# Order of w_in steps, reciprocals and sums in couples 1 to 6 of a fused attention and feed-forward kernel

## The chip, the cores and the metric

The kernel runs on one core of a Trainium2 chip. The metric is the device time of one execution in microseconds (us). Engines are called TensorE (PE in the profile; PEld is its weight load), VectorE (DVE), ScalarE (ACT), GpSimd (POOL) and SyncE (SP, which issues most DMAs).

## What is computed

```
q, k, v: (8, 12, 448, 64) float32;  g_q, g_k: (64,)
q_n = q / sqrt(mean(q*q) + 1e-6) * g_q;   k_n likewise
attn = softmax(q_n @ k_n^T / 8);          o = attn @ v
x = o, heads side by side                 # (3584, 768)
h = x @ w_in;  out = silu(h) @ w_out      # w_in (768, 2048), w_out (2048, 768)
```

w_in and w_out arrive with 8 bytes per element and are rounded to 4 on the chip.

## The kernel before, in words

**Couples.** Two pairs of heads (four heads of one batch) make a couple. There are NC = 24 couples; the code counts them c = 0 to 23, so "couple 1" in the title is c = 0 and "couple 6" is c = 5. GROUP = 6 couples hold two batches, after which the products with w_in for those two batches can run. EARLY is 5, LATE 12, LEFT 3: the 448 keys are three blocks of 128 (j = 0, 1, 2) and a rest of 64 per head (j = LEFT).

**Order.** Nothing is scheduled by a planner. The order of the program text is the order in each engine's queue; an instruction waits by semaphores for its inputs and for the readers of what it overwrites. `visit(c)` writes out the attention of couple c: `scores` (TensorE, then the exponential on ACT, L714), `weigh` (exponentials times v, L746), `add` (DVE, L760: adds blocks of exponentials for the softmax sum). It starts with the end of couple c - 1: `weigh` of its LEFT and last blocks, then a copy of the two results out of PSUM into x (L1393), or from c - 1 = 5 on `divide` at once. `beside` is the RMS normalisation of couple c + 1, in four pieces: squares on ACT (L464), reductions on DVE (L465), roots and scaling on POOL (L493, L508).

`between(c)` follows: q transposes of c + 1 (`transpose_q`, L626), the softmax sums of c (`sum_up`, products with ones, L780, into one PSUM tile `t`), k transposes of c + 1 (`transpose_k`, L644), and `fill`, which deals out products of the feed-forward part (L882) with other work between them.

**Reciprocals.** `sum_up` yields twice: after the first block's products, and with a list of two steps when all sums are issued. The steps are `invert(0)` and `invert(1)`, one reciprocal on DVE for each half of `t` (L789, into r[0]), and `spread`, six DMAs that copy rows of r so that both pairs' factors are in place: four (L795) that read what invert wrote, then two (L797) that overwrite part of what these read, and so wait for them. `divide` multiplies x by r (L804). For c = 0 to 2 these steps are kept in `inverting` and run in the middle of visit(c + 1), after the division of couple c - 1. For c = 3 and 4 they are dealt out in the second `fill` of between(c), after the division of c - 1. For c = 5 they run in between(5), also after it.

**PSUM.** Eight banks: "sc", two tiles of two banks (scores and transposes, in turn); "av0" and "av1", one bank each (sums of `weigh`); "mm", two tiles of one bank (feed-forward products; `bank` hands them out). The tile `t` of `sum_up` comes from `bank` for c < 6, and from "sc" after that.

**w_in.** `Rounder` takes 24 pieces of 128 x 512 through load (DMA), `open` (two ACT instructions, L100 and L101) and `round` (three on DVE, L123 to L130, one add on POOL, L134, and up to two further loads). `weights_in(c, half)` gives the steps of a half couple, "r" for a rounding and "o" for an opening; it also gives calls of `sum_w_in(i, step)`, one DVE operation on 128 x 768 (L837 or L840) that builds sums of blocks of w_in for a seven-product scheme. Chunk 0 needs its four steps before the products of between(6).

**Early products.** `make_ahead`, begun in between(3), computes two products each for the first two row blocks (L882); they are dealt out in five shares, one in between(3) and two each in between(4) and between(5). A product of `mm` is copied by ACT (L890) or added by DVE (L840) before its bank is free.

**SP's queue** in a couple: the q load (L268), `spread`, "vrest" loads (L326, L329), the v load for the next couple (L313), k loads (L289, L293), w_in loads (L85).

Of the kernel before, what the change touches and what calls it, by code (L numbers as in the profile page):

```python
# [11 lines left out]
F32 = mybir.dt.float32  # L12
# [15 lines left out]
BANK = 512  # L28
# [504 lines left out]
def bounded(  # L533
# [3 lines left out]
    P, D, R, J, S = z.P, z.D, z.R, z.J, z.S  # L537
# [5 lines left out]
    ps = others.enter_context(tc.tile_pool(name="ps", bufs=1, space=bass.MemoryType.PSUM))  # L543
# [3 lines left out]
    GROUP, LATE = z.NPAIR, z.LATE  # L547
# [152 lines left out]
    def scores(c, j, i=None):  # L700


        two = ps.tile([P, 2, BANK], F32, name="sc", bufs=2)
        for half in range(2):
            pair = half if j == LEFT else i
            keys = kT[:, ds((z.KA, z.KB)[0 if j == LEFT else i] + j * P, P)]
            for h in range(2):
                rows = ds(h * D, D)
                nc.tensor.matmul(  # L709
                    two[ds(half * D, D), h, 0:S], keys[rows, ts(half, D)], qT[rows, pair, :],  # L710
                    start=True, stop=True,
                )
        for h in range(2):
            nc.scalar.activation(  # L714
                eleft[:, h] if j == LEFT else weights(c, j)[:, i, h], two[:, h, 0:S], AF.Exp,
                scale=norm.column(c, i, h, j),
            )
# [46 lines left out]
    def sum_up(c):  # L764

        n = D // 2
        early = c < GROUP  # L770
        t = bank(S) if early else ps.tile([P, 2, BANK], F32, name="sc", bufs=2)[:, 0, 0:S]
        terms = [(0, lambda: weights(c, 0))]
        if early:
            terms = [(0, lambda: weights(c, LEFT - 1))] + terms + [(1, None)]
        for k, (which, w) in enumerate(terms):
            if k == len(terms) - 2:
                yield
            for h in range(2):
                for i in range(2):
                    nc.tensor.matmul(  # L780
                        t[ds(h * D + i * n, n), :],
                        ones[:, which + i if which else 0],
                        eleft[:, h] if which else w()[:, i, h],
                        start=(k == 0), stop=(k == len(terms) - 1),
                    )

        def invert(half):
            rows = ts(half, S // 2)
            nc.vector.reciprocal(out=r[0][:, rows], in_=t[:, rows])  # L789

        def spread():
            mine = [a.rearrange("(h i p) s -> i h p s", h=2, i=2) for a in r]
            for i in range(2):
                for h in range(2):
                    nc.sync.dma_start(mine[1][i, h], mine[0][1, h])  # L795
            for h in range(2):
                nc.sync.dma_start(mine[0][1, h], mine[0][0, h])  # L797

        yield [lambda: invert(0), lambda: (invert(1), spread())]

    def divide(c, source):
        for i in range(2):
            x = x_of(c, i)
            nc.vector.tensor_tensor(  # L804
                out=x, in0=x if source is None else source[i], in1=r[i], op=ALU.mult
            )
# [55 lines left out]
    def bank(n):  # L862
        turn = turns["next"] = (turns["next"] + 1) % 4
        if ps_alone is None or turn == 0:
            return ps_mm.tile([P, BANK], F32, name="mm")[:, 0:n]
        return ps_alone.tile([P, BANK], F32, name="alone")[:, 0:n]
# [486 lines left out]
    step_of = {"o": lambda: room.w_in.open(), "r": lambda: room.w_in.round()}  # L1353
    halves = {0: "ro", 1: "ro", 2: "ro", 3: "roo", 4: "or", 5: "or", 6: "or", 7: "oroo"}
    visits = {GROUP + 2: "rr", GROUP + 4: "rr"}
    sums_halves = {-6: [(0, 0)], -5: [(0, 1)], -4: [(0, 2)], -3: [(0, 3)]}
    sums_halves[8] = [(3, step) for step in range(4)]
    sums_visits = {GROUP + 1: 1, GROUP + 3: 2}

    def weights_in(c, half):  # L1360
        i = 2 * (c - GROUP) + half
        work = [step_of[step] for step in ("ro" if c < GROUP else halves.get(i, ""))]
        return work + [lambda a=a: sum_w_in(*a) for a in sums_halves.get(i, ())]

    def weights_in_visit(c):
# [9 lines left out]
    def visit(c):  # L1375

        beside = normalise(c + 1) if c <= GROUP else []
        if c < NC:
            scores(c, 0, 0)
        run_all(beside[0:1])  # L1380
        if c > 0:
            weigh(c - 1, LEFT)
            weigh(c - 1, LEFT - 1, 0)
            turn(1, nc.scalar.copy if c <= GROUP else nc.vector.tensor_copy)
        if c < NC:
            scores(c, 0, 1)
        if c == 0:
            run_all(beside[1:2])
        if c > 0:
            weigh(c - 1, LEFT - 1, 1)  # L1390
            if c - 1 < EARLY:
                for i in range(2):
                    nc.vector.tensor_copy(x_of(c - 1, i), sums[i])  # L1393
                run_all(beside[1:2])
                if inverting:
                    if c > 1:
                        divide(c - 2, None)
                    run_all(inverting)
                    inverting.clear()
            else:  # L1400
                divide(c - 1, sums)
                run_all(beside[1:2])
                if c < NC and c % GROUP == 0:
                    for i in range(0 if c == GROUP else 1, HW):
                        sum_x(last_two(c), i)
                weights_in_visit(c)
            if c + 1 < NC:
                loads["vrest"](c + 1)
        if c == NC:
            return  # L1410
        scores(c, 1, 0)
        scores(c, 1, 1)
        if c < GROUP:
            run_all(beside[2:3])
        weigh(c, 0, 1)
        scores(c, 2, 0)
        weigh(c, 1, 1)
        turn(0, nc.scalar.copy)
        if c < GROUP:
            run_all(beside[3:4])  # L1420
        scores(c, 2, 1)
        weigh(c, 0, 0)
        run_all(add(c, 1))
        weigh(c, 1, 0)
        scores(c, LEFT)
        if c + 1 < NC:
            loads["v"](c + 1)

    def run_all(work):
        for piece in work:  # L1430
            piece()

    def between(c):

        def transposes_and_sums():
            summing = sum_up(c)
            if c < GROUP:
                next(summing)
            if c < LATE - 1:
                transpose_k(c + 1)  # L1440
            reciprocals = next(summing)
            if LATE - 1 <= c < NC - 1:
                reciprocals += [lambda: flip(c + 1, "k"), gain]
            if GROUP // 2 <= c <= EARLY:
                divide(c - 1, None)
            return reciprocals

        if c < LATE - 1:
            transpose_q(c + 1)
        elif c < NC - 1:  # L1450
            flip(c + 1, "q")
        if c < GROUP // 2:
            inverting.extend(transposes_and_sums())
        elif c == GROUP - 1:
            run_all(transposes_and_sums())
        if c >= GROUP and c % GROUP == 0:
            fetched = range(AHEAD) if c == GROUP else ()
            columns = products - 2 * HW * S * len(fetched)
            work = halves_in(last_two(c), range(HF), plain_in, dict(begun), fetched)
            begin(work, columns, 2 * GROUP)  # L1460
            begun.clear()
        late = add(c, LEFT - 1) + add(c, LEFT) if c >= GROUP else []
        further = normalise(c + 2) if c >= GROUP - 1 else []
        fill(late + weights_in(c, 0) + further[2:])
        prompt = transposes_and_sums() if GROUP // 2 <= c != GROUP - 1 else []
        if c == GROUP // 2:
            begin(make_ahead([0, 1]), AHEAD * 2 * HW * S, GROUP - 1)
        if c >= LATE - 2:
            if c == LATE - 2:
                prompt.append(pair_up)  # L1470
            queries = prompt[3:] + [lambda: sum_squares(c + 2)]
            fill(weights_in(c, 1), prompt[:3] + [lambda: run_all(queries)])
        else:
            fill(weights_in(c, 1) + (further[:2] if c >= GROUP else []), prompt)
        if c % GROUP == GROUP - 1:
            finish()
            if c == GROUP - 1:
                begun[0] = fetch_ahead([0, 1], 0)
            else:
                sum_x([c // GROUP * 2, c // GROUP * 2 + 1], 0)  # L1480
        if c >= LATE - 2:
            scale(c + 2)
        if GROUP <= c < NC - 1:

            nc.scalar.activation(first, minus_half, AF.Exp)
        if c == NC - 1:
            while rounder.load():
                pass

    begun, inverting = {}, []  # L1490
# [234 lines left out]
```

## Time and profile before

| | us |
|---|---|
| median of 3 runs | 1331.43 (1331.42 to 1336.38) |
| profiled execution, whole time | 1333.6 |
| its span | 1331.8 |
| TensorE busy | 1301.7 (98%) |
| DVE busy | 942.2 (71%) |
| ACT busy | 506.6 (38%) |
| POOL busy | 363.8 (27%) |

The span is what the profiler saw of the program; the whole time is 1.8 us longer. Busy shares are averages over the whole span: attention of the first six couples takes about the first 130 us, a stretch without the large feed-forward products. In timelines a row has its start, its duration, the engine, the line, the operation with what it writes and reads, and in brackets the idle time before it and what ended it. Merged rows ("x2") cover several instructions. "Q" after an engine (SPq) marks what its instruction queue does, such as issuing DMAs.

### The profile page before, as it was taken

Reading aid. Unit: us, or ns where it says so; the run is one execution under the profiler, and the core shown is the slowest. Engines: PE = TensorE matmul, PEld = TensorE weight load, DVE = VectorE, ACT = ScalarE, POOL = GpSimd, SP = SyncE. Lnnn points to the kernel's source line nnn. Section 1 sums busy time; section 2 is a strip of 40 time slices with the busy share of each in tenths; the row PEclk is TensorE's granted clock in tenths of the full one; section 3 lists DMA queues with packets and bytes.
Section 4 is the critical chain, followed back from the end, with each engine's and each line's share of the span. In section 5 each row is a group of like instructions: output and inputs, shape, how many; then the busy total and the mean of one; then the engine's idle time right before and its main releaser. Section 6 shows DMA issues by size and latency. Waiting matters only on the chain.

```text
span 1331.8 us, 19793 instructions
## 1 busy us (share of the span) xinstructions
PE 1301.7 (98%) x7189; PEld 833.1 (63%) x7189; DVE 942.2 (71%) x1623; ACT 506.6 (38%) x890; POOL 363.8 (27%) x229
## 2 busy tenths in 40 slices
PE   8998999999999999999999999999999999999998
PEld 4333444444444444444444455557999999999998
DVE  5787777785755555854554586688978787878785
ACT  7876556655454554455545244410001000001000
POOL 5765534344333433433330154410000000000000
PEclk9999999999999999999999999999999999999999
DMA  8564436333444444444321257522323232332311
GB/s 231 149 167 134 119 98 168 103 89 94 95 94 115 98 93 117 94 94 115 88 66 62 97 179 249 171 74 76 99 76 99 76 105 83 97 105 71 127 48 39
DMA packets 249487, 144.94 MB, mean 109 GB/s; under 512 B 184292, under 2 KB 233316, under 8 KB 249380
## 3 DMA queue, kind: packets, MB, share of 16 engines
q1 hardware_dynamic: 248816, 142.60, 38.0%
q8 instruction: 59, 0.97, 0.3%
q0 software_dynamic: 256, 0.79, 0.2%
q14 instruction: 48, 0.39, 0.1%
q10 hardware_dynamic: 308, 0.20, 0.1%
HBM read 93.98 MB, written 41.29 MB: 102 GB/s over the span
## 4 chain that ended last, share of the span: by engine, by line
PE 84%; DVE 7%; ACT 3%; issue 3%; DMA 2%; POOL 1%; SPq 0%; ACTq 0%; DVEq 0%; POOLq 0%
PE mm L882 26%; PE alone L1189 22%; PE av L746 8%; PE sc L709 7%; PE mm L1189 7%; PE alone L882 7%; PE alone L1226 2%; DVE work L760 1%; PE sc L780 1%; DVE work L789 1%; DVE sums_x L837 1%; DMA work<-work 1%; PE mm L1226 1%; PE sc L644 1%; PE sc L626 0%
## 5 line engine op out<-in xcount | busy, mean ns | idle before, releaser
L882 PE MATMUL mm<-x,W 128*128 128x448 f32 x636 | 256.7, 546 | 6.1 <-DVE parts L840 2.3
L714 ACT ACTIVATE work<-sc,rms 128x448 f32<-128x448 f32 x324 | 184.7, 633 | 81.0 <-PE sc L709 64.9
L882 PEld LDWEIGHTS mm<-x,W 128*128 128x128 f32 x636 | 116.7, 190 | 138.0 <-issue 109.0
L882 PE MATMUL mm<-sums_x,W 128*128 128x448 f32 x456 | 183.7, 543 | 1.6 <-DVE parts L840 1.6
L709 PE MATMUL sc<-work 64*64 64x448 f32 x1344 | 168.2, 549 | 2.6 <-ACT work L714 1.4
L746 PE MATMUL av<-work,rows 64*64 64x448 f32 x1296 | 156.6, 543 | 6.3 <-ACT av L722 1.8
L760 DVE TENSOR_TENSOR work<-work 128x896 f32<-128x896 f32 (+1 forms) x114 | 123.7, 1118 | 49.3 <-PE av L746 48.7
L493 POOL TENSOR_TENSOR rms<-rms,minus_half 128x14 f32<-128x14 f32 (+4 forms) x43 | 106.4, 2476 | 149.8 <-DVE rms L489 140.2
L882 PEld LDWEIGHTS mm<-sums_x,W 128*128 128x128 f32 x456 | 85.1, 190 | 90.7 <-issue 82.8
L520 POOL DMA_DIRECT2D out_dram<-x x2 | 1.3, 653 | 443.2 <-DVE x L840 443.2
L1189 PE MATMUL alone<-W,rows 128*128 128x192 f32 x608 | 113.0, 326 | 0.0
L746 PEld LDWEIGHTS av<-work,rows 64*64 64x64 f32 x1296 | 59.9, 133 | 78.0 <-issue 35.5
L709 PEld LDWEIGHTS sc<-work 64*64 64x64 f32 x1344 | 55.2, 134 | 73.8 <-ACT work L714 27.6
L1189 PEld LDWEIGHTS alone<-W,rows 128*128 128x128 f32 x608 | 101.2, 190 | 0.0
L902 POOL TENSOR_TENSOR parts<-parts,stage 128x448 f32<-128x448 f32 x31 | 42.0, 1356 | 148.7 <-DVE parts L840 148.4
L685 POOL TENSOR_TENSOR rms<-rms,minus_half 128x28 f32<-128x28 f32 x12 | 57.5, 4794 | 67.2 <-DVE rms L682 58.0
L1189 PE MATMUL alone<-W,work 128*128 128x192 f32 x382 | 72.2, 326 | 0.0
L1020 ACT ACTIVATE stage<-stage 128x896 f32<-128x896 f32 x63 | 57.3, 945 | 24.1 <-DVE stage L840 23.4
L465 DVE TENSOR_REDUCE rms<-rows 128x8 f32<-128x512 f32 (+2 forms) x56 | 35.9, 641 | 42.5 <-ACT rows L464 38.9
L1189 PEld LDWEIGHTS alone<-W,work 128*128 128x128 f32 x382 | 63.8, 190 | 0.0
L1199 ACT COPY rows<-alone 128x192 f32<-128x192 f32 x34 | 10.8, 317 | 137.8 <-PE alone L1189 79.0
L789 DVE RECIPROCAL work<-sc 128x224 f32<-128x224 f32 x36 | 55.7, 1548 | 5.2 <-PE sc L780 5.0
(244 smaller groups left out, 2115.4 us busy)
## 6 DMA issues: line engine op xcount, KB each, us to landing
hidden<-stage SPq DMA_DIRECT2D x63, 448.0 KB, 3.0
work<-hidden SPq DMA_DIRECT2D x21, 1024.0 KB, 5.0
rows<-in_moe_w_out_dram SPq DMA_DIRECT2D x32, 384.0 KB, 3.3
W<-in_moe_w_in_dram SPq DMA_DIRECT2D x22, 512.0 KB, 5.2
work<-work SPq DMA_DIRECT2D x144, 56.0 KB, 2.0
x<-hidden SPq DMA_DIRECT2D x7, 1024.0 KB, 6.1
rows<-in_q_dram SPq DMA_DIRECT2D x96, 56.0 KB, 2.2
rows<-in_k_dram SPq DMA_DIRECT2D x96, 56.0 KB, 2.3
```

Of the source, the lines that this page charges most:

```text
L493: nc.gpsimd.tensor_tensor(out=t, in0=t, in1=half, op=ALU.pow)
L685: nc.gpsimd.tensor_tensor(out=f, in0=f, in1=minus_half.to_broadcast([P, n]), op=ALU.pow)
L709: nc.tensor.matmul(two[ds(half * D, D), h, 0:S], keys[rows, ts(half, D)], qT[rows, pair, :], start=True, stop=True,)
L714: nc.scalar.activation(eleft[:, h] if j == LEFT else weights(c, j)[:, i, h], two[:, h, 0:S], AF.Exp, scale=norm.column(c, i, h, j),)
L746: nc.tensor.matmul(sums[i][ds(h * D, D), :], v, w, start=(j == 0 and step == 1), stop=(j == LEFT - 1 and step == 1),)
L760: nc.vector.tensor_tensor(out=total, in0=total, in1=more, op=ALU.add)
L789: nc.vector.reciprocal(out=r[0][:, rows], in_=t[:, rows])
L882: nc.tensor.matmul(t, self.left(name, s), self.right(name, s), start=s == ends[0], stop=s == ends[1])
L902: nc.gpsimd.tensor_tensor(out=u2, in0=u2, in1=p5, op=ALU.add)
L1020: nc.scalar.activation(t, t, AF.Silu)
L1189: nc.tensor.matmul(t, x[:, i], y, start=i == ORDER[0], stop=i == ORDER[-1])
L1226: nc.tensor.matmul(o, a[:, 2 * i + m, t], right_one(name, i)[:, m], start=n == 0, stop=n == len(steps) - 1,)
```

## The change

Six edits, all of which act on c = 0 to 5:

- For c = 0 to 2, one opening of w_in moves into visit(c), ahead of `scores(c, LEFT)`; the two halves of between(c) then have two roundings ("rr") and one opening ("o") instead of "ro" twice.
- The steps in `inverting`, with the division that goes ahead of them, move from the middle of visit(c) to its end, after `add(c, 1)` and `scores(c, LEFT)` and ahead of the v load.
- The tile `t` of the softmax sums comes from "sc" for c = 3 to 5 too.
- The four `sum_w_in` steps of chunk 0 move from c = 3 and 4 (one in each half) to the second half of c = 4 (one), the first half of c = 5 (two) and its second half (one).
- `spread` issues its four copies by h first, then i, and for c = 5 issues those of h = 1 from POOL.
- In between(5) all sums and the list of reciprocals come ahead of the k transposes.

```
-        t = bank(S) if early else ps.tile([P, 2, BANK], F32, name="sc", bufs=2)[:, 0, 0:S]
+        if c < GROUP // 2:
+            t = bank(S)
+        else:
+            t = ps.tile([P, 2, BANK], F32, name="sc", bufs=2)[:, 0, 0:S]
...
-            for i in range(2):
-                for h in range(2):
-                    nc.sync.dma_start(mine[1][i, h], mine[0][1, h])
+            queues = (nc.sync, nc.gpsimd if c == GROUP - 1 else nc.sync)
             for h in range(2):
-                nc.sync.dma_start(mine[0][1, h], mine[0][0, h])
+                for i in range(2):
+                    queues[h].dma_start(mine[1][i, h], mine[0][1, h])
+            for h in range(2):
+                queues[h].dma_start(mine[0][1, h], mine[0][0, h])
...
-    sums_halves = {-6: [(0, 0)], -5: [(0, 1)], -4: [(0, 2)], -3: [(0, 3)]}
+    for c in range(GROUP // 2):
+        halves[2 * (c - GROUP)], halves[2 * (c - GROUP) + 1] = "rr", "o"
+    sums_halves = {-3: [(0, 0)], -2: [(0, 1), (0, 2)], -1: [(0, 3)]}
...
-        work = [step_of[step] for step in ("ro" if c < GROUP else halves.get(i, ""))]
+        work = [step_of[step] for step in halves.get(i, "ro" if c < GROUP else "")]
...
                 run_all(beside[1:2])
-                if inverting:
-                    if c > 1:
-                        divide(c - 2, None)
-                    run_all(inverting)
-                    inverting.clear()
...
         weigh(c, 1, 0)
+        if c < GROUP // 2:
+            room.w_in.open()
         scores(c, LEFT)
+        if inverting:
+            if c > 1:
+                divide(c - 2, None)
+            run_all(inverting)
+            inverting.clear()
         if c + 1 < NC:
             loads["v"](c + 1)
...
             if c < GROUP:
                 next(summing)
+            if c == GROUP - 1:
+                reciprocals = next(summing)
             if c < LATE - 1:
                 transpose_k(c + 1)
-            reciprocals = next(summing)
+            if c != GROUP - 1:
+                reciprocals = next(summing)
```

## The prediction

> **What bounds the kernel now.** Code counts couples from 0, so "couple 6" is c = 5; visit(c) and between(c) are the two halves of a couple, spread(c) the six copies of its reciprocals. I read the page first:
>
> ```profile
> span 1331.8 us, 19793 instructions
> ...
> PE 1301.7 (98%) x7189; PEld 833.1 (63%) x7189; DVE 942.2 (71%) x1623; ACT 506.6 (38%) x890; POOL 363.8 (27%) x229
> ...
> PE   8998999999999999999999999999999999999998
> ```
>
> TensorE is busy for 98% of the span, and 30.1 us are left. The 40 slices show them at the start; after 150 us nothing of this change acts. So a gain is bounded by TensorE's pauses in the first 150 us, while a new pause there has no limit and shifts everything behind it. Second view, TensorE's waits from 20 to 131 us (total, times, longest):
>
> ```profile
> PE av L746 <- ACT av L722: 1.8, 3, 1.4
> PE av L746 <- DVE x L804: 1.8, 1, 1.8
> PE sc L644 <- ACT work L714: 1.4, 2, 1.2
> PE mm L882 <- DVE stage L840: 1.3, 1, 1.3
> PE av L746 <- DVE x L1393: 1.1, 1, 1.1
> PE av L746 <- DMA rows<-in_v_dram: 1.1, 1, 1.1
> PE mm L882 <- ACT stage L890: 0.6, 1, 0.6
> ```
>
> They sum to 9.1 us; each is a hand-over from DVE, ACT or a load. The stretches give one thing more (columns: stretch; PE, PEld, DVE, ACT, POOL busy; clock; DMA share; GB/s): after the 1.81 us pause that ends at 130.89, TensorE runs at half clock, so that pause costs about 1.7 us again.
>
> ```profile
> 132.50:135.70 3.20, 3.20 (x20) 1.43 (x14) 3.13 (x7) 1.32 (x3) 3.12 (x2) 0.50 0.31 68
> ```
>
> Third view, the timelines of SP, DVE and TensorE around c = 2 and 3, on which the forecast rests:
>
> ```profile
> 65.23 0.60 SPq L313 DMA_DIRECT2D rows<-in_v_dram  x1
> ...
> 72.29 2.48 SPq L795 DMA_DIRECT2D work<-work  x4
> 75.75 2.43 SPq L797 DMA_DIRECT2D work<-work  x2
> ```
>
> ```profile
> 79.69 1.16 DVE L804 TENSOR_TENSOR x<-x,work 128x448 f32<-128x448 f32 x2 [1.81 <-DMA work<-work]
> 80.76 1.55 DVE L789 RECIPROCAL work<-mm 128x224 f32<-128x224 f32 x1
> ...
> 84.56 1.55 DVE L789 RECIPROCAL work<-mm 128x224 f32<-128x224 f32 x1
> ...
> 86.77 1.15 DVE L1393 COPY x<-av 128x448 f32<-128x448 f32 x2
> ```
>
> ```profile
> 80.80 0.98 PE L709 MATMUL sc<-work 64*64 64x448 f32 x8
> ```
>
> Reciprocals of c = 2 end on DVE at 72.26; their copies land at 79.69, 7.4 us later, and only then can DVE divide couple 2 and go on to the reciprocals of c = 3 (second half done at 86.1). TensorE meanwhile starts visit(4) at 80.80, undisturbed, because the sums of c = 3 sit in a bank of "mm".
>
> [...] DVE stood idle 1.81 us before the division with the reciprocals of c = 3 queued behind. [...] Here 1.8 us of pause was enough, with half clock for about 3.4 us. [...]
>
> **The change, part by part.** Times are on the old clock until a shift is named.
>
> *w_in steps, c = 0 to 2.* An opening is two ACT instructions, L100 and L101, 0.59 + 0.59 = 1.2 us. One moves into the visit ahead of the LEFT exponentials, where ACT idles 1.2 us (before 22.21 and 39.76): free; were the gap gone, it would cost 1.2. In between(0) two openings instead of three precede visit(1): -1.1 of the 1.38 us pause at 30.96; before visit(2) -0.2. The second rounding (three DVE operations, 1.55 us; one on POOL, 1.3) follows earlier, beside TensorE; same loads on SP.
>
> *Reciprocals of c = 0 to 2 to the end of visit(1) to (3).* The step issues two divisions (1.1 us, from c = 1), two reciprocals (2.95) and six SP copies (4 x 0.58, then 2 x 0.5 behind waits). On DVE it passes the two k reductions and add(c, 1). That frees the LEFT exponentials of visit(2), which waited 2.83 us for add: -1.2 at L644 (58.56) and -0.2 after it. On SP it passes only the three "vrest" loads and stays ahead of the v load.
>  Visit(1): add ends at 39.2 (shift included), reciprocals 42.1; copies issue to 44.6, the last two to 47.2, v at 47.25. Usable 3.0 later (as 65.23 to 68.20): 50.2, where TensorE wants it at 49.72 - 1.3 = 48.4: +1.8.
>  Visit(2): add to 56.7, division 57.8, reciprocals 60.75; v at 65.9, usable 68.9, wanted at 66.15: a pause of 2.75 in place of 1.14: +1.6.
>  So far -1.1 - 0.2 + 1.8 - 1.4 + 1.6 = +0.7.
>
> *Visit(3) into visit(4): the main term.* Add(3, 1) waits for the k squares (ACT ends 71.67): with +0.7 it runs 73.15 to 75.2; division 76.3; reciprocals of c = 2 end at 79.2, not 72.26. One rounding later, at 80.8, DVE meets the division of couple 2 and waits for spread(2): 79.2 + 7.1 = 86.3. Then division 1.1, reciprocal 1.5, rounding 1.5, reciprocal 1.5: 91.9 (the sum of weights between them, 0.87, has left). The sums of c = 3 now use an "sc" tile, of which there are two. LEFT, q, sums, k, next scores alternate, so scores(4, 0) takes the sums' tile and waits for both reciprocals. TensorE is there at 81.5 and starts at about 91.9: **+10.4**. The old 1.14 us pause for L1393 goes: -1.1. After such a pause I take one half-clock window: +1.7 (0 to 3.4).
>
> *Sums of c = 4 in "sc".* The 1.29 us pause at 101.65 (product waiting for its "mm" bank) goes, but scores(5, 0) waits for the second reciprocal at 105.45, where it would start at 102.06: 3.4 in place of 1.29: +2.1, and a half-clock window: +1.7 (0 to 1.7).
>
> *Couple 6 and the sums of weights.* The sums run ahead of k: four transposes' worth, 0.9 us, so reciprocals end near 121.6, not 122.5. In "sc" they are read before scores(6, 0) at 123.5: free; the L890 pause goes: -0.6. Two queues: SP's half lands near 127; for POOL I take the issue of its row (0.55 to 0.76) and landings of 2.2 (1.9 to 4.7): near 127.6, instead of 130.2. Behind POOL's wait stand the rounding's add, the k roots and another add (1.3 + 2.6 + 1.3); POOL's gap of 2.81 us before 132.30 takes that. But three sums of weights (3 x 0.87 = 2.6) now lie on DVE between the reciprocals and the division: 121.6 + two roundings 3.1 + sums 2.6 + reductions and L840 2.6 = 129.9. The division starts 0.3 earlier than at 130.21, against a TensorE that is 0.6 earlier; pause and half clock stay: -0.4 (-3.5, if all of both went, to +2).
>
> Sum: 0.7 + 10.4 - 1.1 + 1.7 + 2.1 + 1.7 - 0.4 = **+15.1 us**. The profiled execution took 1333.6 (span 1331.8 and 1.8 around it): 1348.7. The median of runs, 1331.43, lies 2.2 lower: **1346.5**.
>
> **Rivals.**
> *Faster: the exponentials decide.* If spread(2) is on time, the old pauses simply go: 1.1 + 0.2 + 1.4 + 1.3 + 0.6 + 1.8 + 1.7 = 8.1, 1323.3. For it: ACT's 2.83 us wait behind add. Its point: the reciprocals of c = 2 must end by 72.3 and the second of c = 3 by 80.8. Against: add itself runs past that.
> *Near the bound: only the copies wait.* If scores(4, 0) is not held by the sums' tile, TensorE meets the late DVE first at the av copies (L1393): 91.2, less 0.7 + 86.1 where it would be, so +4 to +5 with 1.7 of half clock and none of c = 4's: 1337.
> *No change: loads only.* The DVE wait is hidden and gains pay for the v loads: 1331.
> *Not as described:* POOL's copies are no faster than SP's; DVE arrives at 129.9 anyway, so 0 to +2; inside the range.
>
> **Numbers.** 0.5% is 6.7 us, about what a measurement here can tell from no change: 1324.8 to 1338.1. Main case 0.77, copies only 0.10 (half of it beyond the bound), no change 0.08, faster 0.05 (most of it beyond). Low end 1335: the copies-only case. High end 1353: main case with spread(2) at 9.1 us, as spread(3) took (+2), half clock also in visits 2 and 3 (+1.7 each) and one more window. Faster 0.03, same 0.15, slower 0.82.
>
> **What would show it.** Right: TensorE's waits gain one of 8 to 12 us, scores L709 on DVE's L789, near 82 us, and one of about 3 before visit(5); DVE's L804 of c = 2 waits 5 us or more for copies; v pauses twice, near 48 and 66; L644's wait is gone; half clock after the long pause. Wrong: visit(4) starting before 86; the long wait at L746 on L1393 (copies only); no wait over 2 us before 110 (faster). A pause near 130 under 0.5 would say that I overcharged the moved sums.

## The result: 0.7% slower, and the profile after

The changed kernel takes 1343.38 us (median of 6 runs, 1342.26 to 1344.99) against 1331.82 for the kernel before beside it (6 runs, 1331.42 to 1336.38): a ratio of 1.0073, 95% interval 1.006 to 1.0087. (This is not the ratio of the two medians, which is 1.0087.) The profiled execution of after took 1344.99 us, its span is 1343.2, so the spans of the two profiles differ by 11.4 us.

The page of the changed kernel:

```profile
span 1343.2 us, 19812 instructions
...
PE 1306.8 (97%) x7189; PEld 835.2 (62%) x7189; DVE 945.2 (70%) x1623; ACT 507.3 (38%) x890; POOL 362.1 (27%) x232
...
PE   8979899999999999999999999999999999999998
```

The instructions of TensorE are the same in number. It is busy for 5.1 us longer and idle for 6.3 us longer (36.4 in place of 30.1). The third slice of 33 us has fallen to 7. So the time went in the part that the change touches, in pauses and, for the busy part, in matmuls that ran slower.

TensorE's waits of the changed kernel from 20 to 145 us (total, times, longest):

```profile
PE sc L709 <- DVE work L792: 3.4, 1, 3.4
PE av L746 <- DVE rms L465: 3.0, 1, 3.0
PE av L746 <- DVE x L808: 2.7, 1, 2.7
PE av L746 <- DMA rows<-in_v_dram: 2.6, 1, 2.6
PE av L746 <- ACT av L722: 0.8, 2, 0.6
PE sc L709 <- ACT work L714: 0.7, 2, 0.5
```

Four pauses of 2.6 to 3.4 us stand where the kernel before had none above 1.81. The waits for L644 and for the early products have gone, as forecast, and so has all but 0.3 us of that for L1393. (Lines from 780 on are numbered 3 to 6 higher in the changed kernel: L780 is L783, L789 is L792, L804 is L808, L1393 is L1399.) TensorE's timeline shows where the four stand:

```profile
50.74 1.77 PE L746 MATMUL av<-work,rows 64*64 64x448 f32 x8 [2.58 <-DMA rows<-in_v_dram]
...
70.66 1.49 PE L746 MATMUL av<-x,rows 64*64 64x448 f32 x8 [3.00 <-DVE rms L465]
...
85.08 0.98 PE L709 MATMUL sc<-work 64*64 64x448 f32 x8
...
89.67 0.98 PE L709 MATMUL sc<-work 64*64 64x448 f32 x8 [0.53 <-ACT work L714]
94.00 0.98 PE L709 MATMUL sc<-work 64*64 64x448 f32 x8 [3.35 <-DVE work L792]
95.27 2.29 PE L746 MATMUL av<-work,rows 64*64 64x448 f32 x8 [0.29 <-DVE x L1399]
...
138.88 1.54 PE L746 MATMUL av<-work,rows 64*64 64x448 f32 x6 [2.65 <-DVE x L808]
```

Visit(4) begins at 85.08 without a wait, and only its fourth scores meet the reciprocals. ACT's exponentials of the first and the second scores:

```profile
86.19 1.16 ACT L714 ACTIVATE work<-sc,rms 128x448 f32<-128x448 f32 x2 [0.47 <-PE sc L709]
...
88.45 1.16 ACT L714 ACTIVATE work<-sc,rms 128x448 f32<-128x448 f32 x2 [0.52 <-PE sc L709]
```

They end at 87.35 and 89.61, and the second and third scores begin at 87.41 and 89.67. So the first three scores used one of the two "sc" tiles in turn, while the sums held the other until 93.94.

TensorE's rows show the second loss too: behind these pauses eight matmuls take 1.5 to 2.3 us (six take 1.54 behind the last), 0.98 in the other rows. The stretches behind the four pauses (stretch; PE, PEld, DVE, ACT, POOL busy; clock; DMA share; GB/s):

```profile
50.70:54.10 3.40, 3.36 (x20) 1.43 (x24) 0.34 (x1) 0.02 (x1) 2.22 (x2) 0.52 0.92 218
...
71.20:74.60 3.40, 3.40 (x24) 1.51 (x20) 0.00 (x0) 0.89 (x2) 2.18 (x2) 0.53 0.88 225
...
95.10:98.50 3.40, 3.23 (x18) 2.04 (x22) 2.10 (x5) 1.65 (x3) 3.32 (x3) 0.53 0.78 227
...
139.50:142.90 3.40, 3.40 (x24) 1.55 (x24) 3.33 (x5) 0.13 (x1) 3.40 (x3) 0.53 0.23 54
```

Each has one window of 3.4 us at half clock (0.52 or 0.53 over the stretch, whose start lies 0.2 us behind the window's), which by my estimate costs half of it, 1.7 us. A fifth follows a pause of 2.01 us at 234.13 (0.54 from 235.10 to 238.50), where the kernel before paused 1.10 at full clock (1.00 from 220 to 240). So there are five windows in place of one. Four times 1.7 is 6.8 us, an upper estimate: TensorE's busy time, which holds the slower matmuls, grew by 5.1 us. The windows are those of the profiled execution. Its mean granted clock was 0.993, and the other five runs had 0.993 to 0.995.

SP and DVE of the changed kernel, where the delay starts:

```profile
47.44 0.53 SPq L313 DMA_DIRECT2D rows<-in_v_dram  x1
...
67.27 0.53 SPq L313 DMA_DIRECT2D rows<-in_v_dram  x1
...
82.48 2.47 SPq L799 DMA_DIRECT2D work<-work  x4
85.17 1.72 SPq L801 DMA_DIRECT2D work<-work  x2
```

```profile
79.50 2.96 DVE L792 RECIPROCAL work<-mm 128x224 f32<-128x224 f32 x2
...
88.38 1.16 DVE L808 TENSOR_TENSOR x<-x,work 128x448 f32<-128x448 f32 x2 [4.46 <-DMA work<-work]
89.46 1.55 DVE L792 RECIPROCAL work<-sc 128x224 f32<-128x224 f32 x1
92.39 1.55 DVE L792 RECIPROCAL work<-sc 128x224 f32<-128x224 f32 x1
```

The v loads are issued 3.3 and 3.4 us before TensorE uses them, so they come last at 50.74 and 70.66. The trace names a reduction (L465) at 70.66, which had nothing to do with v; the experiment with v first shows that it was the load. Reciprocals of c = 2 end at 82.46 instead of 72.26; DVE then stands 4.46 us before the division of couple 2, with the reciprocals of c = 3 queued behind, and these end at 93.94, when TensorE goes on.

### The profile page after: what moved, and what is told of

It is laid out like the page before. It is cut to its first block, busy times and chain, and to the rows that moved or that the text cites. A ratio compares the mean times of both kernels' runs of the same rounds, so it can differ in the third digit from the quotient of the medians.

```text
span 1343.2 us, 19812 instructions
## 1 busy us (share of the span) xinstructions
PE 1306.8 (97%) x7189; PEld 835.2 (62%) x7189; DVE 945.2 (70%) x1623; ACT 507.3 (38%) x890; POOL 362.1 (27%) x232
## 4 chain that ended last, share of the span: by engine, by line
PE 83%; DVE 7%; ACT 4%; issue 3%; DMA 2%; POOL 1%; SPq 0%; ACTq 0%; DVEq 0%; POOLq 0%
PE mm L886 25%; PE alone L1193 22%; PE av L746 8%; PE sc L709 8%; PE mm L1193 7%; PE alone L886 7%; PE alone L1230 2%; PE sc L783 1%; DVE work L760 1%; DVE sums_x L841 1%; DVE work L792 1%; PE mm L1230 1%; DVE rms L465 1%; ACT stage L1024 1%; ACT L1024 1%
## 5 line engine op out<-in xcount | busy, mean ns | idle before, releaser
L714 ACT ACTIVATE work<-sc,rms 128x448 f32<-128x448 f32 x324 | 184.8, 633 | 88.5 <-PE sc L709 75.7
L709 PE MATMUL sc<-work 64*64 64x448 f32 x1344 | 169.3, 556 | 6.6 <-DVE work L792 3.4
L746 PE MATMUL av<-work,rows 64*64 64x448 f32 x1296 | 157.6, 551 | 7.9 <-DVE x L808 2.7
L746 PEld LDWEIGHTS av<-work,rows 64*64 64x64 f32 x1296 | 60.7, 135 | 80.5 <-issue 40.7
L709 PEld LDWEIGHTS sc<-work 64*64 64x64 f32 x1344 | 55.4, 135 | 80.7 <-ACT work L714 29.1
L792 DVE RECIPROCAL work<-sc 128x224 f32<-128x224 f32 x42 | 64.8, 1547 | 7.4 <-PE sc L783 7.2
L465 DVE TENSOR_REDUCE rms<-rows 128x8 f32<-128x512 f32 (+2 forms) x56 | 36.0, 643 | 46.7 <-ACT rows L464 45.1
```

The lines of the kernel that those rows point to most:

```text
L465: nc.vector.tensor_reduce(out=out, in_=t.rearrange("p (n d) -> p n d", n=n), axis=AX.X, op=ALU.add)
L709: nc.tensor.matmul(two[ds(half * D, D), h, 0:S], keys[rows, ts(half, D)], qT[rows, pair, :], start=True, stop=True,)
L714: nc.scalar.activation(eleft[:, h] if j == LEFT else weights(c, j)[:, i, h], two[:, h, 0:S], AF.Exp, scale=norm.column(c, i, h, j),)
L746: nc.tensor.matmul(sums[i][ds(h * D, D), :], v, w, start=(j == 0 and step == 1), stop=(j == LEFT - 1 and step == 1),)
```

## The experiments

Ratios are to the kernel before, on the same chip, with 95% intervals. The kernel before had medians of 1333.4, 1333.0 and 1333.9 us in the three groups.

| run | ratio | interval |
|---|---|---|
| e1_undo_move | 0.9996 | 0.9987 to 1.0005 |
| e2_v_first | 1.0031 | 1.0019 to 1.0042 |
| e3_sums_mm | 1.0078 | 1.006 to 1.0096 |
| e4_sums_w_back | 1.0062 | 1.0044 to 1.0081 |
| e5_move_only | 1.0079 | 1.0063 to 1.0096 |
| e6_sums_w_back_one_queue | 1.0055 | 1.0038 to 1.0072 |
| e8_all_but | 0.9973 | 0.9966 to 0.998 |
| e9_vrest_last | 0.9976 | 0.9969 to 0.9984 |
| g1_k_after_sums | 0.9963 | 0.995 to 0.9976 |
| g2_two_queues | 0.9968 | 0.9958 to 0.9979 |
| g3_sums_w_late | 0.9998 | 0.9992 to 1.0005 |
| g4_steps_only | 0.9976 | 0.9967 to 0.9984 |

**Is it the move of the reciprocals?** From the changed kernel with the move undone:

```
                 run_all(beside[1:2])
+                if inverting:
+                    if c > 1:
+                        divide(c - 2, None)
+                    run_all(inverting)
+                    inverting.clear()
...
         scores(c, LEFT)
-        if inverting:
-            ...
```

> The changed kernel with one part undone: division and reciprocals of couples 1 to 3 run in the middle of the visit again. Theory (their move to the end of the visit makes the v loads and DVE late, and the pauses halve the clock): the v pauses of 2.6 and 3.0 us, the scores wait of 3.4 us on the reciprocals and three half-clock windows go; the opening in the visit keeps its 1.2 us gain; 1327 to 1331, below the 1331.8 of before. Rival (the sums' PSUM tile and couple 6 carry the loss, the move is neutral): 1340 or more.

And the kernel before with the move alone (the same edit the other way round):

> The kernel before with only the division and reciprocals of couples 1 to 3 moved to the end of the visit. Theory (the move is the loss): v pauses near 49 and 68 us of 2 to 3 us each with half clock, and DVE late at the copies out of av in visit 4 (about 4 to 5 us, L1393): 1341 to 1345. Rival (the move costs only together with the sums in sc): 1334 to 1337.

Undone, the whole loss goes: 1332.59 us, ratio 0.9996. The gain below the kernel before that was expected besides doesn't show. Alone, the move costs all of it: 1342.86 us, 1.0079. So the other five edits sum to about nothing; what they hide from each other is taken apart below. In the second kernel the sums of c = 3 are in "mm", and nothing holds the scores; TensorE runs on to the weigh that needs L1393's copy and waits there. Its timeline:

```profile
52.40 0.98 PE L746 MATMUL av<-work,rows 64*64 64x448 f32 x8 [2.39 <-DMA rows<-in_v_dram]
...
70.59 0.98 PE L746 MATMUL av<-x,rows 64*64 64x448 f32 x8 [2.36 <-DMA rows<-in_v_dram]
...
94.67 2.29 PE L746 MATMUL av<-work,rows 64*64 64x448 f32 x8 [5.84 <-DVE x L1393]
```

Both v loads are late here too, and their pauses of 2.4 us are followed by full clock (0.98 for eight matmuls), the 5.84 us one by slow matmuls for some 4.5 us (2.29, 2.23 and 2.01 us for eight), more than the 3.4 us of one window.

**The v loads.** From the changed kernel, the v load goes ahead of the moved block:

```
+        if c + 1 < NC:
+            loads["v"](c + 1)
         if inverting:
...
             inverting.clear()
-        if c + 1 < NC:
-            loads["v"](c + 1)
```

> The changed kernel with the v load issued ahead of the moved reciprocals instead of behind their copies. Theory: both pauses at the first product with v (2.6 and 3.0 us) and their two half-clock windows go, about -9 us; the wait of the scores on the reciprocals of couple 4 (3.4 us, with a half-clock window) stays, because DVE still waits for the copies of couple 3; 1334 to 1337. Rival (the record names a DVE reduction, L465, as what ended the second pause, so DVE is late, not v): the second pause stays, 1339 to 1341. Second rival (the pauses only cover later waits): 1342 to 1344.

1337.74 us, 1.0031: 0.7 us above the range expected, on a chip where the kernel before took 1.6 us longer than in the first comparison. In the profile both v pauses have gone, and the two half-clock windows behind them (eight matmuls of L709 or L746 take 0.98 us at most from 41 to 82 us); the wait on the reciprocals is where it was. (The profiled run, 1335.32 us, is the shortest of the seven, at a granted clock of 0.996. The others had 0.993 to 0.995. One window of 3.4 us at half clock lowers the mean over 1333.5 us by 0.0013, so by my estimate they kept one or two windows more than it shows.) Its timeline of TensorE:

```profile
86.05 1.77 PE L709 MATMUL sc<-work 64*64 64x448 f32 x8 [3.56 <-DVE work L792]
```

So about 0.42% (1.0073 less 1.0031), some 5.6 us, came of v loads queued behind six copies on SP; the two intervals leave room for roughly 3 to 8 us. As the move costs the whole loss, the 0.31% left is put down to the late DVE, by difference; no run took that part out alone.

**Does the "sc" tile matter?** From the changed kernel:

```
-        if c < GROUP // 2:
+        if early:
             t = bank(S)
```

> The changed kernel with the sums of couples 4 to 6 back in a bank of mm. Theory (DVE is late, and the tile only decides where TensorE meets it): the 3.4 us wait of the scores at 94 goes, but TensorE then waits about as long for the copies out of av; and the pauses of 1.3 us (product before visit 5) and 0.6 us come back: 1343 to 1346. Rival (holding the sc tile is the cost): the wait and one half-clock window go without a substitute: 1338 to 1340.

1344.17 us, 1.0078: nothing gained. The wait moves from the scores to the next weigh (TensorE's timeline):

```profile
92.34 1.55 PE L746 MATMUL av<-work,rows 64*64 64x448 f32 x6 [4.83 <-DVE x L1399]
```

The wait is longer, 4.83 us in place of 3.35, because with the tile free TensorE gets there sooner. From the visit's first scores to this weigh it is 10.3 us (82.02 to 92.34), as against 10.2 in the changed kernel (85.08 to 95.27). The tile is not the cause: DVE is late, and TensorE meets it at the tile or, one step on, at the copy of the results.

**Sums of weights and the second queue, in the changed kernel.** The sums of chunk 0 back where they were:

```
-    sums_halves = {-3: [(0, 0)], -2: [(0, 1), (0, 2)], -1: [(0, 3)]}
+    sums_halves = {-6: [(0, 0)], -5: [(0, 1)], -4: [(0, 2)], -3: [(0, 3)]}
```

> The changed kernel with the four sums of weights back in couples 4 and 5. Theory A (as predicted: the sums of weights on DVE between the reciprocals and the division of couple 6 take the gain of the earlier copies): the 2.65 us pause near 138 shrinks by 2.6 us or more and its half-clock window goes: 1338 to 1340. Theory B (the copies of couple 6 land at 137.1, only 1.1 us before DVE reaches the division): the pause shrinks by 1 us at most, half clock stays, and couple 4's DVE chain gets 0.9 us longer: 1342.5 to 1344.

1342.47 us, 1.0062: about 1.5 us less, which the overlapping intervals don't establish. The pause before the weigh of couple 6 falls from 2.65 to 2.05 us and keeps its half clock (two matmuls take 0.96 us behind it), as theory B had it. In addition, all copies on SP:

```
-            queues = (nc.sync, nc.gpsimd if c == GROUP - 1 else nc.sync)
+            queues = (nc.sync, nc.sync)
```

> The variant with the sums of weights back in couples 4 and 5, where DVE waits 2.7 us for the copies of couple 6, with all six copies on SP. Theory ([...] the second queue saves issue time that is hidden): the division waits as long within 0.5 us, POOL's roundings and scaling come 3 to 4 us earlier and the pauses at the q transposes (0.8 us) go: 1341 to 1342.5. Rival (two queues save 1.2 us of issue and one wait): the division comes 1.2 to 2 us later: 1343.5 to 1345.

1339.87 us, 1.0055, below both ranges expected; the pause before the weigh is 1.42 us here, without half clock (0.54 for two matmuls). The division of couple 6 begins 7.4 us after its reciprocals end with one queue, 8.1 with two: POOL's queue brought the copies no earlier. As these kernels carry the long pauses too, both questions were asked again without the move.

**The rest without the move.** The kernel before with the w_in steps, the sums of c = 3 to 5 in "sc" and the copies' order, and nothing else of the change:

> The kernel before with the w_in steps of couples 1 to 3 and the sums of couples 4 to 6 in sc; the reciprocals, the sums of weights and couple 6's order and queue as before. Theory (these two parts are the gain that was hidden): pauses of 1.2 and 0.2 us in visits 1 and 2, 1.3 us before visit 5 and 0.6 us before visit 6 go, the pause before visit 4 falls from 1.1 to 0.5: 3 to 4 us below before, 1328.5 to 1330.5. Rival (pauses move on to later waits): within 1 us of before.

1329.66 us (20 runs), 0.9973: faster than both kernels. In its profile no half-clock window is left from 14 to 150 us (eight matmuls of L709 or L746 take 1.22 us at most, against 1.5 to 2.3 in the slow rows of the changed kernel). With the "vrest" loads behind the v load too, in visits 1 to 5:

```
-            if c + 1 < NC:
+            if c >= GROUP and c + 1 < NC:
                 loads["vrest"](c + 1)
...
+            if 0 < c < GROUP:
+                loads["vrest"](c + 1)
```

> The same, and in visits 1 to 5 the three vrest loads are issued behind the v load instead of ahead of it. Theory (SP's queue delays v in visit 2): v is issued 2 us earlier and the 1.1 us pause near 65 us goes: 1 us below the variant without this, 1327.5 to 1329.5. Rival (v waits for the copies of the reciprocals, which stay ahead, or the k loads behind become late): no change.

1329.55 us, 0.9976: no gain. The pause of 1.73 us near 66 goes, but one of 1.94 comes at 72.18 (sums waiting for ACT's L714), with half clock behind it (seven k transposes take 1.43 us, 0.98 in e8_all_but).

The w_in steps and the copies' order alone, with the sums in "mm":

> The kernel before with the steps of w_in in another order for c = 0 to 2 alone (and the copies' order h first, then i, on SP). Theory: the gain of e8_all_but, about 3.6 us, has two parts: the steps give 1.2 to 1.4 (less of the pause before visit(1), 0.2 before visit(2)), the sums of c = 3 to 5 in sc give the rest; so 1331.5 to 1332.5 against about 1333 of the kernel before. Rival (all from the steps, by half-clock windows gone): 1329.5. Second rival (all from the sums): 1333.

1330.22 us, 0.9976. The first rival is right: the whole gain comes with the steps, and the "sc" tile adds nothing that shows. I had priced the steps at 1.3 us; 3.2 came. With the earlier start the division of couple 2 waits 1.01 us instead of 1.81 and L1393 is on time, and the pause of 1.81 near 131 is 1.19 and has no half clock after it (0.54 for two matmuls, 0.96 in the kernel before). How much of this is the order of the copies (the last two take SP 1.70 us in place of 2.43) was not separated.

**Couple 6's three edits, one at a time**, on e8_all_but. First the sums ahead of the k transposes:

```
+            if c == GROUP - 1:
+                reciprocals = next(summing)
             if c < LATE - 1:
                 transpose_k(c + 1)
-            reciprocals = next(summing)
+            if c != GROUP - 1:
+                reciprocals = next(summing)
```

> e8_all_but with the sums of c = 5 ahead of the k transposes, one queue. Theory (the order k loads, copies decides): the reciprocals end 0.9 us earlier (four transposes' worth), but SP then issues the k loads just ahead of the copies, whose landing grows from about 1.9 to 4 us, so the division of c = 5 does not come earlier; the pause of 1.67 us ahead of the weigh at 126 stays between 1.4 and 2.5 us, time 1329 to 1331. Rival (the copies wait only for the reciprocals): the division comes 0.9 us earlier, the pause falls to about 0.8, time 1328.5 or, with a half-clock window less, 1327.

1328.79 us, 0.9963. DVE's timelines, e8_all_but first:

```profile
115.60 2.97 DVE L792 RECIPROCAL work<-sc 128x224 f32<-128x224 f32 x2 [2.34 <-PE sc L783]
...
125.38 1.21 DVE L808 TENSOR_TENSOR x<-av,work 128x448 f32<-128x448 f32 x2 [1.28 <-DMA work<-work]
```

```profile
113.33 2.97 DVE L792 RECIPROCAL work<-sc 128x224 f32<-128x224 f32 x2 [1.14 <-PE sc L783]
...
123.28 1.21 DVE L808 TENSOR_TENSOR x<-av,work 128x448 f32<-128x448 f32 x2 [1.45 <-DMA work<-work]
```

DVE's wait for the sums falls by 1.2 us, and from the end of the reciprocals to the division it is 6.81 and 6.98 us. My theory, that k loads issued just ahead would hold the copies up, is refuted; the rival holds, and TensorE's pause falls from 1.67 to 0.99. In time the step from 0.9973 to 0.9963 is within the intervals. It has the lowest median of all kernels run.

The second queue:

```
-            queues = (nc.sync, nc.sync)
+            queues = (nc.sync, nc.gpsimd if c == GROUP - 1 else nc.sync)
```

> e8_all_but with POOL issuing the copies of h = 1 for c = 5. Theory: each copy lands no earlier from a second queue; POOL's own work stands behind the wait of its last copy for 3 to 4 us, so the q transposes' waits on POOL (1.1 us in e8) grow by 0.5 to 1; division of c = 5 within 0.7 us of e8's 125.4; time 1329.5 to 1332. Rival (the issue time of SP decides): the division comes 1.2 us earlier, the pause at 126 falls under 0.6, time 1328.

1330.38 us, 0.9968: no difference to e8_all_but that shows. The division starts 6.77 us after the reciprocals end (6.81 with one queue), and POOL's next work waits for its last copy. Its timeline of POOL, and of TensorE:

```profile
117.97 1.22 POOL L799 DMA_DIRECT2D work<-work  x2 [4.26 <-DVE W L123]
122.30 0.50 POOL L801 DMA_DIRECT2D work<-work  x1 [3.11 <-DMA work<-work]
```

```profile
132.91 0.60 PE L626 MATMUL sc<-ident,rows 112*128 112x112 f32 x4 [1.63 <-POOL rows L508]
```

The q transposes then wait 1.63 us for POOL's L508, which e8_all_but doesn't have there; the theory holds.

The sums of weights at c = 4 and 5:

```
-    sums_halves = {-6: [(0, 0)], -5: [(0, 1)], -4: [(0, 2)], -3: [(0, 3)]}
+    sums_halves = {-3: [(0, 0)], -2: [(0, 1), (0, 2)], -1: [(0, 3)]}
```

> e8_all_but with the four sums of weights moved to the second half of c = 4 and both halves of c = 5, as in the changed kernel. Theory: three sums (2.6 us of DVE) lie between the reciprocals of c = 5 and its division, where DVE waits only 1.28 us for copies in e8; so the division comes 1.3 us later, the pause at 126 grows from 1.67 to about 3, at half clock afterwards; time 1331 to 1333.5. Rival (DVE has room elsewhere before the division): hidden, 1329.5.

1333.65 us, 0.9998: 3.4 us more than g4_steps_only on the same chip, whose ratio is that of e8_all_but. The size is the theory's (a little over its upper end), the place is not. Its timelines of DVE, ACT and TensorE:

```profile
119.44 2.91 DVE L841 TENSOR_TENSOR W<-W 128x768 f32<-128x768 f32 x2
122.27 0.67 DVE L465 TENSOR_REDUCE rms<-rows 128x8 f32<-128x512 f32 x1
...
127.04 1.15 DVE L808 TENSOR_TENSOR x<-av,work 128x448 f32<-128x448 f32 x2
```

```profile
122.98 0.63 ACT L464 ACTIVATE rows<-rows 112x512 f32<-112x512 f32 x1 [2.24 <-DVE rms L465]
123.51 0.15 ACT L722 COPY av<-minus_half 128x1 f32<-128x1 f32 x1
```

```profile
123.72 1.67 PE L746 MATMUL av<-work,rows 64*64 64x448 f32 x8 [2.36 <-ACT av L722]
```

The sums push the k reduction back; ACT's next squares wait 2.24 us for it by the trace; the small copy L722 stands behind them in ACT's queue, and the weigh needs it. A half-clock window follows (clock 0.53 from 123.70 to 127.10). The division, 8.99 us after the reciprocals, waits for no copy and is no longer met. The path to TensorE was a reduction and ACT's queue, not the division. Late sums lose about what the w_in steps bring (0.9998 against 0.9973, and 0.9976 against 1), which fits the 0.9996 of e1_undo_move.

## Why the prediction was right in its total and wrong in its main term

1346.5 was forecast, 1343.38 came, inside the range. By the starts of the same TensorE rows before and after, in order of time:

| part | forecast | measured |
|---|---|---|
| up to scores(4, 0): 80.80 to 85.08 | +0.7 | +4.3 |
| visit(4), to the q transposes: 93.47 to 102.52 | +10.4 - 1.1 + 1.7 = +11.0 | +4.8 |
| c = 4, to scores(5, 0): 103.35 to 110.85 | +2.1 + 1.7 = +3.8 | -1.5 |
| couple 6, to L882: 139.41 to 148.56 | -0.4 | +1.6 |
| after that | 0 | +2.2 |
| sum | +15.1 | +11.4 |

- **w_in steps: right** here (30.96 to 29.75, -1.2 for -1.1), too small by themselves, as g4_steps_only shows.
- **v loads: right in cause, too small.** Issue forecast at 47.25, measured 47.44; usable 3.3 us later, not 3.0; pauses 2.58 and 3.00 instead of 1.8 and 2.75. The failed step is the clock: I put half clock in visits 2 and 3 into the upper end alone, and it came after both (3.4 of the 4.3 us). In the runs here pauses of such length had it or had it not (last section).
- **The main term: right in cause, wrong in the resource.** Reciprocals late, the division of couple 2 waiting 4.46 us (forecast 5 or more), the second reciprocal of c = 3 at 93.94 (91.9, and 3.4 us of half clock ahead of it): all this came. The failed step is "scores(4, 0) takes the sums' tile". The tiles didn't alternate, and the fourth scores took it. From 85.08 to 90.65 TensorE did its own work (0.53 us of waiting for ACT in it), and 3.35 us of the lateness were left. My own test, "visit(4) starting before 86", said wrong. The rival "only the copies wait" had this part better: e3_sums_mm and the move alone show its wait at 4.83 and 5.84 us for its +4 to +5. It came to 1337, as it too left out half clock in visits 2 and 3 (3.4 us) and what couple 6 and the time after 150 cost beyond the forecast (4.2 us).
- **c = 4: wrong, same step.** In visit(5) no scores row waits for DVE. The 1.29 us pause of the early product went as forecast, and nothing took its place.
- **Couple 6: term mis-sized.** DVE's and POOL's rows of the changed kernel:

```profile
130.56 1.81 DVE L841 TENSOR_TENSOR W<-W 128x768 f32<-128x768 f32 x2
...
135.60 2.10 DVE L841 TENSOR_TENSOR W<-W 128x768 f32<-128x768 f32 x1
...
138.22 1.14 DVE L808 TENSOR_TENSOR x<-av,work 128x448 f32<-128x448 f32 x2
```

```profile
129.47 1.22 POOL L799 DMA_DIRECT2D work<-work  x2 [3.06 <-DVE W L123]
135.06 0.50 POOL L801 DMA_DIRECT2D work<-work  x1 [4.38 <-DMA work<-work]
135.58 1.30 POOL L134 TENSOR_TENSOR W<-W 128x512 int32<-128x512 int32 x1
```

That the sums of weights eat what the earlier sums give was right: the division follows without a wait for the copies, 9.1 us after the reciprocals. But the three sums took 3.9 us, not 2.6: the third 2.10 instead of 0.95, as POOL's L134 had begun 0.02 us before it. POOL's queue stood 4.38 us behind its copy, more than the 2.81 us gap that I had for cover. So the pause before the weigh grew from 1.81 to 2.65, and the q transposes waited 0.98 more for POOL. By themselves late sums lose (g3_sums_w_late) and the second queue brings nothing (g2_two_queues). Of the three edits only the sums ahead of k shortened the pause, from 1.67 to 0.99 us; that this saves time is not established.
- **After 150: wrong.** I let nothing act there; a pause at 234 grew from 1.10 to 2.01 with a half-clock window. Why it grew was not traced. In the other twelve kernels this pause takes 0.94 to 1.95 us, so it may not be an effect of the change.

So the total stands on errors that offset each other: 10.4 where 3.35 came, and half clock counted twice where five windows came in place of one. By the table, visit(4) and c = 4 were overcharged by 11.5 us and the other three parts undercharged by 7.8. That these nearly cancel is luck.

## What to carry to other kernels

Steps with waiting DMAs that move later in a queue cost what is queued behind them: here loads for the next stage on one queue and reciprocals for the stage after on another; put the next stage's loads ahead of them. Where an engine is late, ask where the bound engine meets it first, and count the independent work up to there, ahead of charging the whole lateness; freeing that one resource may only move the wait to the next meeting. Count the clock where TensorE may stand idle. In the profiles before and after, half clock came behind pauses of 1.81 us and more and behind none of 1.54 or less; in e5_move_only a pause of 2.39 had none. So in a sum of several such pauses put it into the forecast, not only the upper end. A profile shows the windows of one execution; 37 runs of the kernel before had granted clocks from 0.996 to 1.000.

## What the runs showed of the hardware

- Half clock after short pauses. In the profile of the kernel before the clock is 0.50 once from 14 to 1320 us, for 3.413 us from 132.29; in that of the changed kernel five times, each for 3.413 us, from 50.53, 71.01, 94.90, 139.27 and 234.84. These five starts lie 20.48, 23.89, 44.37 and 95.57 us apart, that is 6, 7, 13 and 28 times 3.413. Counted off from the starts in steps of 3.413 us, the two profiles have 758 stretches from 13 to 1320 us that began at full clock. The six in which TensorE ran no matmul for 1.81 to 3.00 us in sum were followed by half clock, the other 752, with 1.56 us at most, were not. The length of the single pause did not decide: 2.39 us in e5_move_only (52.40), 2.46 in e3_sums_mm (49.33) and 1.91 in g1_k_after_sums (65.43) kept full clock, 0.98 us for eight matmuls. In e1_undo_move two pauses of 1.42 and 0.78 us, at 133.39 and 134.77, have twelve products of 5.79 us behind them; in e8_all_but, with the pause of 0.78 but not that of 1.42, the twelve take 4.69.
- The same pauses with and without. Near 745 us e1_undo_move and the kernel before have the same two pauses, 1.54 and 1.37 us, and e1_undo_move alone has half clock behind them. Rows of e1_undo_move, then the stretch behind them in e1_undo_move and in the kernel before (columns as above):

```profile
742.69 0.98 PE L746 MATMUL av<-work,rows 64*64 64x448 f32 x8 [1.54 <-DVE av L722]
745.04 5.31 PE L886 MATMUL alone<-x,W 128*128 128x448 f32 x9 [1.37 <-DVE x L808]
```

```profile
747.00:750.00 3.00, 3.00 (x7) 1.49 (x6) 2.39 (x5) 0.53 (x1) 0.00 (x0) 0.71 0.04 10
```

```profile
747.00:750.00 3.00, 1.67 (x5) 0.95 (x6) 2.93 (x6) 0.00 (x0) 0.00 (x0) 1.00 0.96 357
```

In e1_undo_move the clock is 0.73 from 744 to 747 us and 0.71 from 747 to 750, so half clock began near 745.4, and by my estimate the 3.413 us ahead of it held 2.1 us of the two pauses. In the kernel before, stretches counted off from its window at 132.29 held 1.54 and 1.37 us. Executions of one kernel differ too: 37 runs of the kernel before, beside the last group, had granted clocks from 0.996 (ten runs, mean 1335.4 us) to 1.000 (seven runs, 1332.4 us).
- VectorE beside GpSimd. Four times in the kernel before, a sum of weights (DVE) begins 0.2 us ahead of POOL's L134 (at 76.92, 83.70, 95.90 and 103.03). The sum takes 0.95 us, as with POOL idle (131.42 in the changed kernel), but L134 takes 1.88 to 1.90, where it takes 1.28 to 1.31 with DVE idle (42.17, 59.90 and 128.21). At 135.60 in the changed kernel L134 had begun 0.02 us earlier: it takes 1.30, and the sum 2.10.
- A second issuing queue brought nothing in couple 6 (g2_two_queues against e8_all_but): 6.77 us from the reciprocals to the division in place of 6.81, though SP's issue of the first copies took 1.20 us instead of 3.35.
